# A scan and a mixer on one core: V in one transfer, and the first 150 steps in another order

## The chip, the core and the metric

The kernel runs on one core of a Trainium2 chip. Its engines each work through a queue of their own: TensorE (PE, with its weight loads shown as PEld), VectorE (DVE), ScalarE (ACT), GpSimd (POOL), and SyncE (SP), which here only issues transfers between memory and the on-chip buffers. An instruction starts when it is at the head of its engine's queue and what it waits for has happened. The metric is the device time of one execution in microseconds, as the median of a few runs.

## What is computed

A state-space scan over 4 batches of 8 heads (768 positions, 32 channels, 16 states) gives y. The mixer then takes y as 4 x 768 x 256.

```python
for c in range(nc):                                  # chunks of 32 positions
    L = exp(cum_i - cum_j) * causal
    y[c] = (C B^T * L) @ x + (C @ state) * exp(cum)
    state = exp(sum(la)) * state + sum_j B_j x_j exp(cum_last - cum_j)
h = x.transpose(0, 2, 1) @ U @ V                     # the mixer's x is y; rank 32 over the 768 positions
u = x + h.transpose(0, 2, 1)
out = u + maximum(u @ w_ch1, 0) @ w_ch2              # 256 -> 1024 -> 256
```

The weights U, V, w_ch1 and w_ch2 arrive as 64-bit numbers and are turned into 32-bit ones on the chip.

## The kernel before

The scan goes by pairs: a pair is 256 positions of one batch, so there are 12 pairs, three to a batch. Pairs 0, 1 and 2 make up batch 0. The mixer of batch 0 can begin when all three are through.

The order of all work is written out by hand: the string PLAN (line 40) is a list of 650 words, and the function follow issues what each word stands for, in that order. No scheduler moves anything afterwards, so the place of a word sets the place of its instructions in every engine's queue, its transfers in SP's queue included. The words that matter here, k being a pair:

- b, x, L, B, X: loads of B and C (bc) and of x of a pair; w and W: loads of a block of w_ch1 or w_ch2; Z and z: loads of V and of U. For a word that begins with B, X, w or L, the first load is held until the last VectorE instruction issued before it has run.
- Q, P: the product of bc with the decays (BC), on POOL for pairs 1 to 3, on DVE for the others. T, V: transposes of BC on PE, and ScalarE copies of them into T and Cm.
- g: the gram products on PE (line 537 for pairs 0 to 2, 547 for the others). m, M: their masks, m for the first two banks, M for the last two; in pairs 0 to 2 the fourth bank goes through ACT (line 563) and POOL.
- s: the state products (line 598). u: the running state S on DVE, and after its second call Sm (line 626), on POOL for pairs 0 to 3.
- n: y's part within the chunk (lines 694 and 704). i, j: y's part from the state (line 672), which needs Sm. y: copies of y into yT. t, O and o: transposes of yT and copies into ytok.
- c0 to c9: conversion of a weight block, four steps each, spread over DVE and ACT (lines 442 and 444). c1 converts U and V together; c0 and c2 give the first quarter of w_ch1, c4, c5 and c3 the others.
- p, q, a: the mixer's low-rank part: p multiplies ytok with U (line 751), q spreads the result (line 759) and makes ps, v makes V's spread form Vs (line 902), a adds h to yT (line 769, then four DVE additions for batch 0).
- U: the first w_ch1 products of batch 0 (line 797, "plain", w1f and yT). F: filler products on PE (line 148) that nothing reads.

Three rules set the waits. PSUM has eight banks, handed out in the order of the words, so a product can wait for a bank until an earlier tile in it has been read. Buffers in the pools raw and att are handed round in the same way. And the loads carry eight completion semaphores in turn, so a load is issued only when the eighth load before it has landed.

Of the kernel before, what the change touches and what calls it, by code (L numbers as in the profile page):

```python
# [39 lines left out]
PLAN = (  # L40
# [46 lines left out]
def kernel(  # L87
# [28 lines left out]
    P = 128  # L116
    NB, NH, S, D = x.shape
    N = B.shape[-1]
    NC = S // P
    NPR = NC // 2  # L120
    DM = NH * D
    RK = moe_U.shape[1]
# [7 lines left out]
    Q = 32  # L130
# [27 lines left out]
    class Kept:  # L158
# [6 lines left out]
        def __getattr__(self, name):  # L165
# [16 lines left out]
        out=a_sb,  # L182
        in_=a.rearrange("(g b) h (c s) -> g (b h c) s", g=2, s=P).rearrange(
            "g r s -> r g s"))
# [4 lines left out]
    def hold(load, until):  # L189

        tc.add_manual_dep(load.ins, until.ins.name, mybir.DependencyInfo(
            mybir.DependencyClass.Sync, mybir.DependencyReason.DATA))

    def begin(**kwargs):
        op = nc.sync.dma_start(**kwargs)  # L195
        if until:
            hold(op, until.pop())
# [26 lines left out]
    UV = const.tile([P, 2, NC * RK], FP32)  # L224
# [8 lines left out]
    w2 = [const.tile([P, NM, DM], FP32R, name=f"w2{i}") for i in range(2)]  # L233
    weights = {}
# [7 lines left out]
    def words_of(dst):  # L242
        p, i, j = dst.shape
        t = raw.tile([P, 2 * WCOLS], INT32, tag="words", name="words", bufs=NWORDS)
        return t[:p, :2 * i * j]
# [11 lines left out]
    U2, V2, w12, w22 = (w.bitcast(INT32) for w in (moe_U, moe_V, moe_w_ch1, moe_w_ch2))  # L257
# [2 lines left out]
    w13 = w12.rearrange("(c p) m -> p c m", p=P)  # L260
    own = {}

    def load_v():
        own["UV"] = words_of(UV)
        weights[1] = UV, own["UV"]
        for q in range(4):
            begin(out=own["UV"][ts(q, Q), 2 * NC * RK:], in_=V2[:, ts(q, 2 * NC * RK)])

    def load_u():
        begin(out=own["UV"][:, :2 * NC * RK].rearrange("p (c r) -> p c r", c=NC),  # L270
                          in_=U2.rearrange("(c p) r -> p c r", p=P))

    def load_w(n):
        if n < 2:
# [13 lines left out]
    def load(k):  # L288
        if k < NB * NPR:
            load_bc(k)  # L290
            load_x(k)

    loads = dict(B=load_bc, X=load_x, w=load_w, b=lambda k, p: load_bc(k, (p,)),
                 x=lambda k, c: load_x(k, (c,)), W=load_w, Z=lambda n: load_v(),
                 z=lambda n: load_u())
    for word in LOADS.split():
        loads[word[0]](*(int(v) for v in word[1:].split(".")))
# [36 lines left out]
    for half in range(2):  # L334
        both = sides[:, half].rearrange("p (g s r) -> p s g r", g=2, s=2)
        for s in range(2):
            nc.gpsimd.tensor_scalar(
                out=both[:, s], in0=same[:, None, :].to_broadcast([P, 2, Q]),
# [10 lines left out]
    for g in range(2):  # L349
# [3 lines left out]
        out=la.rearrange("p b c h -> p b h c"),  # L353
# [577 lines left out]
    def ytokens_kept(k):  # L931
# [9 lines left out]
                 v=spread)  # L941
# [51 lines left out]
```

## Time and profile before

| what | us |
|---|---|
| median of 3 runs | 218.69 |
| lowest and highest run | 217.45 and 219.20 |
| the profiled execution, its own time | 216.94 |
| its span, first to last instruction | 215.1 |

The span is what the views below divide up; the profiled execution's own time has 1.84 us around it. The profiled execution is 0.8% under the median of the runs. Busy times overlap, so they don't add up to the span. In a row of the timeline the two numbers ahead are the start and the length in microseconds, and the brackets at its end hold the engine's idle time before it and what ended it.

### The profile page before, as it was taken

Reading aid. Unit: us, or ns where it says so; the run is one execution under the profiler, and the core shown is the slowest. Engines: PE = TensorE matmul, PEld = TensorE weight load, DVE = VectorE, ACT = ScalarE, POOL = GpSimd, SP = SyncE. Lnnn points to the kernel's source line nnn. Section 1 sums busy time; section 2 is a strip of 40 time slices with the busy share of each in tenths; the row PEclk is TensorE's granted clock in tenths of the full one; section 3 lists DMA queues with packets and bytes.
Section 4 is the critical chain, followed back from the end, with each engine's and each line's share of the span. In section 5 each row is a group of like instructions: output and inputs, shape, how many; then the busy total and the mean of one; then the engine's idle time right before and its main releaser. Section 6 shows DMA issues by size and latency. Waiting matters only on the chain.

```text
span 215.1 us, 6853 instructions
## 1 busy us (share of the span) xinstructions
PE 207.0 (96%) x2912; PEld 180.8 (84%) x2912; DVE 161.3 (75%) x334; ACT 119.9 (56%) x273; POOL 14.5 (7%) x46
## 2 busy tenths in 40 slices
PE   7998699999999999999999999999999999999993
PEld 4666465666676989999899999998999999999993
DVE  4679499999999999968977594497347756636942
ACT  3566567896847695655275527433646357357120
POOL 7463210000000000000000000000000000000000
PEclk9999999999999999999999999999999999999999
DMA  5987899998850035002061010100001000100012
GB/s 87 142 184 106 120 202 316 155 265 110 109 80 3 2 66 111 0 3 76 3 81 21 24 49 3 49 27 6 6 0 49 0 27 0 49 29 0 0 50 100
DMA packets 69519, 14.57 MB, mean 68 GB/s; under 512 B 63792, under 2 KB 67696, under 8 KB 69488
## 3 DMA queue, kind: packets, MB, share of 16 engines
q1 hardware_dynamic: 69488, 14.13, 33.6%
q8 instruction: 23, 0.38, 0.8%
q14 instruction: 8, 0.07, 0.1%
HBM read 10.98 MB, written 3.15 MB: 66 GB/s over the span
## 4 chain that ended last, share of the span: by engine, by line
PE 84%; SPq 5%; DMA 4%; DVE 2%; issue 2%; ACT 1%; DVEq 0%
PE x L797 31%; PE z L797 24%; PE y L797 12%; SPq L195 5%; PE y L704 3%; PE y L672 3%; DMA words<-in_moe_w_ch_dram 3%; PE x L547 2%; PE w L728 2%; PE w L506 2%; DMA bc<-in_C_dram 2%; PE w L598 1%; PE w L751 1%; PE z L547 1%; DVE M L169 1%
## 5 line engine op out<-in xcount | busy, mean ns | idle before, releaser
L169 DVE SCALAR_TENSOR_TENSOR words<-words 128x768 fp32r<-128x768 f32 (+6 forms) x48 | 38.0, 818 | 0.7 <-PE y L797 0.5
L797 PE MATMUL z<-u,w 128*128 128x384 f32 x144 | 32.0, 341 | 0.0
L797 PE MATMUL x<-u,w 128*128 128x384 f32 x144 | 31.7, 338 | 0.0
L797 PEld LDWEIGHTS z<-u,w 128*128 128x128 f32 x144 | 24.3, 188 | 0.3 <-issue 0.2
L797 PEld LDWEIGHTS x<-u,w 128*128 128x128 f32 x144 | 24.3, 188 | 0.2
L802 ACT ACTIVATE x<-x 128x384 f32<-128x384 f32 (+1 forms) x32 | 14.3, 448 | 18.1 <-PE x L797 18.1
L802 ACT ACTIVATE z<-z 128x384 f32<-128x384 f32 (+1 forms) x28 | 12.8, 461 | 16.6 <-PE z L797 16.1
L169 DVE SCALAR_TENSOR_TENSOR words<-x,words 128x384 fp32r<-128x384 f32 x24 | 13.1, 553 | 8.7 <-ACT words L831 8.6
L169 DVE SCALAR_TENSOR_TENSOR words<-z,words 128x384 fp32r<-128x384 f32 x24 | 12.9, 552 | 8.9 <-ACT words L831 8.8
L797 PE MATMUL y<-w,words 128*128 128x256 f32 x144 | 19.3, 281 | 0.0
L797 PEld LDWEIGHTS y<-w,words 128*128 128x128 f32 x144 | 18.4, 189 | 0.1
L797 PE MATMUL x<-w,words 128*128 128x256 f32 x128 | 18.3, 281 | 0.0
L797 PE MATMUL x<-w2c,words 128*128 128x256 f32 x96 | 17.6, 317 | 0.0
L797 PEld LDWEIGHTS x<-w,words 128*128 128x128 f32 x128 | 17.0, 188 | 0.2
L797 PEld LDWEIGHTS x<-w2c,words 128*128 128x128 f32 x96 | 14.9, 189 | 1.1
L831 ACT ACTIVATE words<-x 128x384 fp32r<-128x384 f32 x24 | 11.7, 491 | 6.0 <-PE x L797 5.9
L831 ACT ACTIVATE words<-z 128x384 fp32r<-128x384 f32 x24 | 11.6, 492 | 3.0 <-PE z L797 3.0
L169 DVE SCALAR_TENSOR_TENSOR S<-S,kept,w 128x64 f32<-128x64 f32 x40 | 11.1, 278 | 1.6
L797 PE MATMUL z<-yT,w1f 128*128 128x384 f32 x32 | 11.7, 495 | 0.1
L797 PE MATMUL x<-yT,w1f 128*128 128x384 f32 x32 | 11.1, 489 | 0.0
L672 PEld LDWEIGHTS y<-T,Sm 32*64 32x64 f32 x352 | 8.1, 131 | 2.7 <-issue 2.1
L797 PE MATMUL y<-w2c,words 128*128 128x256 f32 x72 | 10.3, 282 | 0.0
(170 smaller groups left out, 398.4 us busy)
## 6 DMA issues: line engine op xcount, KB each, us to landing
words<-in_moe_w_ch_dram SPq DMA_DIRECT2D x7, 512.0 KB, 6.8
x<-in_x_dram SPq DMA_DIRECT2D x24, 128.0 KB, 3.6
out_dram<-ytok SPq DMA_DIRECT2D x24, 128.0 KB, 1.7
bc<-in_B_dram SPq DMA_DIRECT2D x24, 64.0 KB, 3.0
bc<-in_C_dram SPq DMA_DIRECT2D x12, 128.0 KB, 3.1
words<-in_moe_w_ch_dram SPq DMA_DIRECT2D x2, 256.0 KB, 5.5
words<-in_moe_V_dram SPq DMA_DIRECT2D x4, 48.0 KB, 4.8
words<-in_moe_U_dram SPq DMA_DIRECT2D x1, 192.0 KB, 5.0
```

The lines of the kernel that those rows point to most:

```text
L169: self.last = call(*args, **kwargs)
L195: op = nc.sync.dma_start(**kwargs)
L506: nc.tensor.transpose(out=tp[:, i, v], in_=s["BC"][:, i, c + v].rearrange("p h n -> p (h n)"), identity=ident)
L547: nc.tensor.matmul(out=g[r][cols, c], lhsT=s["T"][rows, 0, c, cols], rhs=s["Cm"][rows, :, :, ts(2 * c + p, Q)].rearrange("r v t i -> r v i ...
L598: nc.tensor.matmul(out=s["A"][p][ts(r, Q), v], lhsT=s["BC"][half, 0, v, 2 * r:2 * r + 2].rearrange("p h n -> p (h n)"), rhs=x_sb[k][half, ...
L672: product = nc.tensor.matmul(out=y[at][ts(r % 2, H), c, ts(p, H)] if light else y[p][ts(r % 2, H), r // 2, c], lhsT=own[ts(r, Q)], rhs=s[" ...
L704: product = nc.tensor.matmul(out=y[p][ts(i, Q), n, c], lhsT=x_sb[k][half, c, h], rhs=s["M"][half, h // 2, c, h % 2], start=fresh(k, p, [i] ...
L728: nc.tensor.transpose(out=t[:, c, g], in_=yT[b][:, g, ts(2 * q + c, P)], identity=ident)
L751: nc.tensor.matmul(out=p[ts(i % 4, Q), h], lhsT=U_sb[:, c], rhs=ytok[b][:, c, h], start=i < 4, stop=True, skip_group_check=True)
L797: nc.tensor.matmul(out=t, lhsT=lhsT, rhs=rhs, start=start, stop=True, skip_group_check=True)
L802: nc.scalar.activation(t, t, AF.Copy, scale=1.0 + EPS)
L831: nc.scalar.activation(gs[j, m // 2][0][:, m % 2], t, AF.Relu, scale=NEAR)
```

## The change

The table of words keeps its 650 words. The words that differ in place begin with the 40th and end with the 210th; nothing is added or taken out. In addition V, which was loaded by four transfers of 32 partitions each, is loaded by one transfer to 128 partitions, so that the program has 96 loads and stores in place of 99. A small function makes the buffer that U and V share, so that either load can come first.

```diff
-    'V1.1.2 b4.0 g0 M0 g1 m0 M1 V2.1.2 F2.1 V2.0.2 s1 b4.1 n0 m1 c2 i0 b4.2 j0 u1.0 b5.1 c0 u1.1 '
+    'V1.1.2 g0 b4.2 b4.1 m0 b4.0 b5.1 M0 g1 M1 m1 V2.1.2 s1 V2.0.2 g2 M2 u1.0 u1.1 c0 w3 P3 b5.2 '
...
+    def words_uv():
+        if "UV" not in own:
+            own["UV"] = words_of(UV)
+            weights[1] = UV, own["UV"]
+        return own["UV"]
+
     def load_v():
-        own["UV"] = words_of(UV)
-        weights[1] = UV, own["UV"]
-        for q in range(4):
-            begin(out=own["UV"][ts(q, Q), 2 * NC * RK:], in_=V2[:, ts(q, 2 * NC * RK)])
+        v = words_uv()[:, 2 * NC * RK:]
+        begin(out=v, in_=V2.rearrange("r (q c) -> q r c", q=4))
 
     def load_u():
-        begin(out=own["UV"][:, :2 * NC * RK].rearrange("p (c r) -> p c r", c=NC),
-                          in_=U2.rearrange("(c p) r -> p c r", p=P))
+        begin(out=words_uv()[:, :2 * NC * RK].rearrange("p (c r) -> p c r", c=NC),
+              in_=U2.rearrange("(c p) r -> p c r", p=P))
```

Line numbers of the changed kernel are higher by four behind this place: 537 becomes 541, and so on.

The loads on SP, where V is issued (x here is that of pair 2, bc that of pair 3):

```order
 L195 DMA words<-in_moe_w_ch_dram 128x2x256 x2
-L195 DMA words<-in_moe_V_dram 32x384 x4
+L195 DMA words<-in_moe_V_dram 128x1x384
 L195 DMA x<-in_x_dram 128x8x32
 L195 DMA bc<-in_B_dram 128x8x16
```

Four rows of V become one, in the same place. All that follows stands three places nearer the head of the queue. Further on, the loads of later pairs and of the weight blocks change places among themselves.

VectorE from the first updates of the state S on, through the masks of pairs 0 to 2 (words<-x and words<-z), the states of pairs 1 and 2 and the first conversions. Before:

```order
L169 SCALAR_TENSOR_TENSOR S<-S,kept,w 128x64 x3
L169 TENSOR_TENSOR words<-z,lower 128x512
L169 TENSOR_TENSOR words<-x,lower 128x512 x2
L169 TENSOR_TENSOR words<-z,lower 128x512
L169 TENSOR_TENSOR words<-x,lower 128x512 x2
L169 TENSOR_SCALAR words<-words 128x256 x2
L169 SCALAR_TENSOR_TENSOR S<-S,kept,w 128x64 x2
L169 TENSOR_SCALAR words<-words 128x256 x2
L169 SCALAR_TENSOR_TENSOR S<-S,kept,w 128x64 x2
L169 TENSOR_TENSOR words<-z,lower 128x512
L169 TENSOR_TENSOR words<-x,lower 128x512 x2
L169 SCALAR_TENSOR_TENSOR S<-S,kept,w 128x64 x3
```

The same stretch now:

```order
L169 SCALAR_TENSOR_TENSOR S<-S,kept,w 128x64 x3
L169 TENSOR_TENSOR words<-x,lower 128x512 x2
L169 TENSOR_TENSOR words<-z,lower 128x512 x2
L169 TENSOR_TENSOR words<-x,lower 128x512 x2
L169 TENSOR_TENSOR words<-z,lower 128x512
L169 SCALAR_TENSOR_TENSOR S<-S,kept,w 128x64 x4
L169 TENSOR_SCALAR words<-words 128x256 x2
L169 TENSOR_TENSOR words<-x,lower 128x512 x2
L169 TENSOR_SCALAR words<-words 128x256 x2
L169 SCALAR_TENSOR_TENSOR words<-words 128x256 x2
L169 SCALAR_TENSOR_TENSOR S<-S,kept,w 128x64 x3
```

The first mask of pair 2 stands ahead of the four state updates of pair 1, and the last state updates of pair 2 (x3) stand behind three rows of conversions and not between them.

TensorE in the same stretch, from behind the grams of pair 2 to the state products of pair 3 (y<-words,x is n, y<-T,Sm is i and j, w<-ident,BC the transposes of pair 3, x, w and z<-ident,yT those of yT). Before, where n and half of the i and j products of pair 0 stand ahead of those grams:

```order
L694 MATMUL y<-words,x 32x128 x16
L672 MATMUL y<-T,Sm 64x64 x8
L598 MATMUL w<-x,BC 32x64 x12
L728 MATMUL x<-ident,yT 128x128 x4
L672 MATMUL y<-T,Sm 64x64 x8
L694 MATMUL y<-words,x 32x128 x16
L672 MATMUL y<-T,Sm 64x64 x16
L506 MATMUL w<-ident,BC 128x128 x4
L728 MATMUL w<-ident,yT 128x128 x4
L598 MATMUL w<-x,BC 32x64 x16
```

And now:

```order
L698 MATMUL y<-words,x 32x128 x32
L676 MATMUL y<-T,Sm 64x64 x28
L602 MATMUL w<-x,BC 32x64 x12
L732 MATMUL x<-ident,yT 128x128 x4
L698 MATMUL y<-words,x 32x128 x16
L510 MATMUL w<-ident,BC 128x128 x2
L676 MATMUL y<-T,Sm 64x64 x16
L148 MATMUL x<-one 128x256
L510 MATMUL w<-ident,BC 128x128 x2
L732 MATMUL w<-ident,yT 128x128 x4
L602 MATMUL w<-x,BC 32x64 x16
```

The grams of pair 2 come ahead of all y products, the products of pairs 0 and 1 follow in one piece, and half of the transposes of pair 3 stand ahead of pair 2's last products; a filler product (L148) that stood much earlier is put between.

14 rows, old and new, of the table PLAN are left out of this document.

## The prediction

> **What bounds the kernel now.** I read the page's head first, then busy time by windows, then the chain of waits up to the first w_ch1 products, then the timeline of each engine from 10 to 33 us.
>
> ```profile
> span 215.1 us, 6853 instructions
> ...
> PE 207.0 (96%) x2912; PEld 180.8 (84%) x2912; DVE 161.3 (75%) x334; ACT 119.9 (56%) x273; POOL 14.5 (7%) x46
> ```
>
> ```profile
> 15.00:20.00 5.00, 4.24 (x148) 3.03 (x140) 4.45 (x14) 2.67 (x8) 1.51 (x3) 1.00 0.69 99
> 20.00:25.00 5.00, 3.81 (x107) 2.92 (x105) 2.33 (x8) 2.24 (x6) 1.72 (x2) 1.00 0.75 125
> 25.00:30.00 5.00, 3.97 (x101) 2.24 (x86) 4.55 (x15) 3.76 (x10) 0.62 (x1) 1.00 0.97 165
> 30.00:32.60 2.60, 2.56 (x81) 2.01 (x80) 2.51 (x7) 1.93 (x7) 0.10 (x1) 1.00 1.04 224
> 32.60:210.00 177.40, 177.36 (x2296) 160.42 (x2297) 137.38 (x265) 101.17 (x224) 0.84 (x8) 1.00 0.25 53
> ```
>
> Columns: the window, its length, busy PE, PEld, DVE, ACT, POOL, then granted clock, DMA share and GB/s. From 32.6 us to 210 us TensorE is idle for 0.04 us at the full clock. What it has to do there isn't changed, so that stretch keeps its length unless a new wait enters it, and what can be won lies before it: between 15 and 32.6 us TensorE is idle for 0.76 + 1.19 + 1.03 + 0.04 = 3.02 us. The question is when the dense stretch begins. The chain of waits shows what it begins behind:
>
> ```profile
> 10.52 5.51 DMA words<-in_moe_w_ch_dram
> ...
> 18.55 3.54 DMA bc<-in_C_dram
> 22.10 2.20 issue
> 24.30 0.53 ACT words L442
> ...
> 32.64 1.56 PE z L797 x4
> ```
>
> SP waits until 16.03 for the first w_ch1 block, since the second half of pair 2's x is the eighth load after it. Then come pair 3's loads, of which C lands at 22.09, then U, and at 24.30 ScalarE starts to convert U and V (the 2.20 us "issue" is it standing there). The plain w_ch1 products begin at 32.64. So the first 32 us are a race of loads, not of TensorE.
>
> **The change, part by part.** *V as one transfer.*
>
> ```profile
> 11.66 2.69 SPq L195 DMA_DIRECT2D words<-in_moe_V_dram  x4
> 14.39 0.43 SPq L195 DMA_DIRECT2D x<-in_x_dram  x1
> ...
> 19.18 0.58 SPq L195 DMA_DIRECT2D words<-in_moe_U_dram  x1
> ```
>
> ```profile
> words<-in_moe_U_dram SPq DMA_DIRECT2D x1, 192.0 KB, 5.0
> ```
>
> Four issues took 2.69 us; one takes 0.43 to 0.58 by its neighbours, and I take 0.55. All loads behind it move up by 2.1 us, x of pair 2 to 12.2. They are also three places nearer in the turn of eight semaphores: x's second half and pair 3's B and C now wait for bc and x loads that have long landed, so C can be issued after four loads of 0.58, at 14.5 in place of 18.55, and U waits for the first w_ch1 block (16.03) and is issued there in place of 19.18. By the same times to landing C lands at 18.1 at the earliest and U at 21.1. At the latest nothing is gained, 22.1 and 24.2, since the 16 DMA engines were also 0.69 busy there and take the bytes in order. I take the middle for C, 20, and 22 for U; up to about 22 either is free, for the reason that follows.
>
> *The grams of pair 2 ahead of the y products, their first mask ahead of pair 1's states, conversions ahead of pair 2's states.*
>
> ```profile
> 15.71 0.48 PE L537 MATMUL x<-Cm,T 32*64 32x256 f32 x1
> ...
> 17.86 1.08 PE L694 MATMUL y<-words,x 128*32 128x128 f32 x32 [0.76 <-DVE S L169]
> ...
> 21.69 0.78 PE L672 MATMUL y<-T,Sm 32*64 32x64 f32 x32
> 23.37 0.66 PE L506 MATMUL w<-ident,BC 128*128 128x128 f32 x4 [0.90 <-POOL BC L490]
> ```
>
> ```profile
> 14.59 0.67 ACT L516 ACTIVATE Cm<-x,slot 128x128 f32<-128x128 f32 x2
> ...
> 25.84 0.60 ACT L510 COPY T<-w 128x512 f32<-128x512 f32 x1
> 26.31 0.86 ACT L516 ACTIVATE Cm<-w,slot 128x256 f32<-128x256 f32 x2
> ```
>
> ```profile
> 14.43 1.28 DVE L169 TENSOR_TENSOR words<-x,lower 128x512 int32<-128x512 int32 x2
> 16.05 0.50 DVE L169 TENSOR_SCALAR words<-words 128x256 int32<-128x256 int32 x2 [0.34 <-DMA words<-in_moe_w_ch_dram]
> ...
> 17.95 0.68 DVE L169 TENSOR_TENSOR words<-z,lower 128x512 int32<-128x512 int32 x1
> 18.55 1.28 DVE L169 TENSOR_TENSOR words<-x,lower 128x512 int32<-128x512 int32 x2
> 19.90 0.92 DVE L169 SCALAR_TENSOR_TENSOR S<-S,kept,w 128x64 f32<-128x64 f32 x3
> ...
> 29.72 0.75 DVE L169 SCALAR_TENSOR_TENSOR words<-words 128x256 f32<-128x256 f32 x2
> ...
> 46.97 1.30 DVE L169 SCALAR_TENSOR_TENSOR S<-S,kept,w 128x64 f32<-128x64 f32 x4
> ```
>
> ```profile
> 20.91 0.62 POOL L626 TENSOR_TENSOR Sm<-S,own 128x192 f32<-128x192 f32 x1 [1.22 <-DVE S L169]
> 22.22 1.10 POOL L490 TENSOR_TENSOR BC<-bc,F 128x512 f32<-128x512 f32 x1 [0.70 <-DMA bc<-in_C_dram]
> ```
>
> The grams need Cm, which ScalarE has ready at 15.26; with the y products of pair 0 behind them TensorE has nothing in the meantime and loses about 0.9 us that it had filled. They start at 15.3 and end by 16.7: before it was 15.71 to 17.10, which is 17.86 less the wait of 0.76, with other products between, so 1.4 is a high price. VectorE, done with six masks at 15.71, now waits 1.0 for them. From 16.7 it has one mask (0.68), four states (1.30), two conversion rows (0.50 each), two masks (1.28), a third conversion row (0.75) and three states (0.92): 5.9 us as rows, and 5.75 with the 0.1 that consecutive rows overlap, so pair 2's states are done at 22.45 and not at 20.82. POOL's Sm follows at 23.1. Pair 3's BC stands ahead of it on POOL: with C at 20 it runs to 21.1 and hides, and only from C at 22 on does it hold Sm. The last half of pair 2's y products goes from 23.1 to 23.6, 1.1 us later than before (21.69 + 0.78 = 22.47).
>
> What is won back is behind that. Before, T3's transposes ended at 24.03, but their copy on ScalarE began at 25.84, behind the conversion of U that began at 24.30. Now U has landed by 22, VectorE comes to it at 22.5, and ScalarE is through with it by 23.6, under pair 2's products. The filler and T3's second half end at 24.4, the copies take 1.33 (25.84 to 27.17), and pair 3's grams start at 25.8 in place of 27.2: **1.4 us earlier**.
>
> *From there to the plain products* the same instructions run as before: four masks, V's split, BC of pair 4, a conversion, ps, the additions to yT. BC of pair 4 moves from behind ps to ahead of it, but both lay before the additions, so the stretch of 5.4 us (27.2 to 32.64) stays, and the products begin at 31.2. BC of pair 4 needs its loads by 29; they move up with the queue.
>
> *In the dense stretch* the order changes up to the 210th word. One place can give time back: pair 5's state products take the bank that t3's transposes had, behind a ScalarE copy that comes later among the new conversions.
>
> ```profile
> 46.46 0.59 ACT L733 COPY ytok<-w 128x512 f32<-128x512 f32 x1
> ```
>
> Nothing waits there now, so the price is between 0 and that copy's 0.59, and I take 0.4, nearer the upper end, since ScalarE has two conversion steps ahead of it. The x and w loads of later pairs are issued earlier than before or held by the same releases; I cost them at nothing, and their cover is the lead that they had. Sum: -1.4 + 0.4 = -1.0 us. The span goes from 215.1 to 214.1, the profiled execution from 216.94 to 215.9, and as a median, which stands at 218.69 against that execution, to 217.7.
>
> **The rivals.** *V on few engines.* The one transfer reads from memory in 4 blocks of 32 rows, where every load before has 32, 96 or 128 as its outermost count. If the four blocks mean four DMA engines, their share of V is 48 KB each and not 12.
>
> ```profile
> GB/s 164 246 246 266 225 205 205 184 287 266 266 266 297 297 266 317 358 358 369 389 420 338 246 328 328 287 185 246 215 185 144 308 174 154 51 82 21 51 21 82
> ```
>
> That is 13 to 15 us. At the 370 GB/s or so of V's time, 23 GB/s for an engine, V takes 2.1 us on them and not 0.5, and all loads behind wait for these four. C then lands about where it did, near 22.1; BC of pair 3 ends at 23.3, Sm behind it at 23.9, pair 3's grams start at 26.6, and of the 1.4 us 0.6 stay: -0.6 + 0.4 = -0.2, a median of 218.5. No run here has such a load, so nothing in the trace speaks for or against it. The Trainium skill states it as a rule: its page "DMA: Bandwidth & Descriptors", section "Why a DMA increments its semaphore by 16 and not by 1", says that a hardware-generated DMA uses the largest number of engines up to 16 that divides the slowest dimension of both sides, which for 4 and 128 gives the four lowest engines. By that rule the sum is this rival's, without it mine; the trace shows neither, and the chance below is for what it would cost here.
>
> *All of the idle goes.* If loads and copies fall so that TensorE never waits between 15 and 32.6 us, 3.0 us go: 215.7. Against it: the new gap of 0.9 at 14.4 and the later Sm.
>
> *Slower: a conversion between the additions.* The next w_ch1 block's first conversion row now stands on VectorE between the two pairs of additions to yT, at about 31.7; before it came behind all four. It needs the block's load.
>
> ```profile
> 27.01 0.75 SPq L195 DMA_DIRECT2D words<-in_moe_w_ch_dram  x1
> ```
>
> ```profile
> words<-in_moe_w_ch_dram SPq DMA_DIRECT2D x1, 512.0 KB, 5.1
> ```
>
> It landed at 32.1. If it comes no earlier, 0.4 is lost; each us past 31.7 holds VectorE's queue and then TensorE's third product. From a landing at 35 on the kernel is slower by 2.2 us, 220.9. I expect it near 30, since its place in the queue is ahead of two more loads than before.
>
> **How the numbers follow.** My forecast, 217.7: 0.45. V on few engines, 218.5: 0.25. No difference at all, 218.7, the gains and the new gap even: 0.07. All idle gone, 215.7: 0.13. Slower by a late block, 220.9: 0.10. About 1% is what a measurement of this kernel can tell from no change: the runs lie 0.8% apart. Below 216.5 lies the case of 215.7 and the edge of mine, 0.17; above 220.9 half and more of the slower case with longer waits, 0.10; within 1% the rest, 0.73. The range from 215.6 to 219.8 takes in the first four cases and leaves out the slower one and what lies beyond the gain.
>
> **What would show it.** Right: pair 3's C landed by 21 and U by 22; POOL's BC of pair 3 ahead of 22; a TensorE gap near 14.4 to 15.3; pair 3's grams near 25.8, the first plain product near 31.2, and no idle behind. Wrong: C at 22 or later with DMA engines unevenly busy (V on few engines); VectorE idle ahead of the row at 31.7 (late block); TensorE idle between 32 and 110 us, which would mean that the new order starves it where I assumed none.

## The result, and the profile after

| what | us |
|---|---|
| before, median of 9 runs (lowest to highest) | 218.69 (217.34 to 220.65) |
| after, median of 9 runs (lowest to highest) | 220.31 (218.79 to 221.42) |
| after / before, with its 95% interval | 1.0106 (1.0077 to 1.0135) |
| the profiled execution, after (before: 216.94) | 220.73 |
| its span, after (before: 215.1) | 219.0 |

The change costs 1.1% of the time: 1.6 us between the two medians, and 2.3 us by the ratio, which leaves out executions over 1.5% slower than the kernel's quickest, as every ratio below does. The forecast was a gain of 1.0 us. Here are the page's head and the busy time by windows after the change, with the windows and columns of the prediction:

```profile
span 219.0 us, 6852 instructions
...
PE 209.3 (96%) x2912; PEld 182.3 (83%) x2912; DVE 161.7 (74%) x334; ACT 120.4 (55%) x273; POOL 14.2 (6%) x46
```

```profile
15.00:20.00 5.00, 3.75 (x114) 2.55 (x106) 3.71 (x10) 2.64 (x9) 1.92 (x5) 1.00 0.60 105
20.00:25.00 5.00, 3.69 (x117) 2.71 (x117) 3.90 (x12) 2.52 (x7) 1.82 (x3) 1.00 0.87 140
25.00:30.00 5.00, 4.43 (x114) 3.23 (x118) 3.49 (x11) 3.78 (x9) 0.37 (x2) 1.00 0.73 99
30.00:32.60 2.60, 2.59 (x79) 1.61 (x75) 2.60 (x8) 1.70 (x6) 0.60 (x1) 1.00 1.05 227
32.60:210.00 177.40, 175.25 (x2306) 157.68 (x2300) 137.63 (x266) 102.42 (x226) 0.90 (x9) 1.00 0.26 54
```

From 32.6 to 210 us TensorE is now idle for 2.15 us in place of 0.04. Fixed windows mix causes, because this execution also reached its first gram product later (11.86 us, against 10.53), and that lies ahead of all that was changed. So I cut both executions at three events of the program instead: the first gram product of pair 0, that of pair 3, the first plain product, the end. Before, then after:

```profile
10.53:27.23 16.70, 13.79 (x392) 9.47 (x391) 11.86 (x31) 10.65 (x30) 6.92 (x13) 1.00 0.81 138
27.23:32.64 5.41, 5.26 (x143) 3.63 (x143) 4.98 (x15) 3.50 (x11) 0.72 (x2) 1.00 0.95 204
32.64:215.10 182.46, 179.22 (x2310) 162.08 (x2310) 138.38 (x267) 101.13 (x224) 0.84 (x8) 1.00 0.26 55
```

```profile
11.86:29.06 17.20, 14.07 (x391) 9.64 (x390) 12.01 (x30) 10.20 (x29) 6.81 (x13) 1.00 0.77 131
29.06:35.43 6.37, 5.31 (x142) 3.65 (x143) 5.23 (x15) 3.47 (x11) 0.72 (x2) 1.00 0.82 169
35.43:219.00 183.57, 179.47 (x2311) 162.10 (x2310) 138.31 (x267) 102.31 (x224) 0.79 (x8) 1.00 0.25 54
```

The three stretches grew by 0.50, 0.96 and 1.11 us, together 2.57, near the 2.3 of the ratio. Of this TensorE is idle for 0.22, 0.91 and 0.86 (length less busy PE), and busy longer by 0.28, 0.05 and 0.25. So the time isn't lost in one place. These are TensorE's waits in the profile after, first those from 14 to 34.4 us, then those from 34 to 205 us (us in total, how many, the longest):

```profile
PE w L510 <- POOL BC L494: 1.1, 1, 1.1
PE x L541 <- ACT Cm L520: 1.0, 1, 1.0
PE x L551 <- ACT Cm L520: 0.6, 1, 0.6
PE x L510 <- DVE words L169: 0.3, 1, 0.3
```

```profile
PE x L773 <- DVE w1f L169: 1.0, 1, 1.0
PE y L676 <- issue: 0.6, 1, 0.6
PE w L510 <- DVE M L169: 0.5, 1, 0.5
```

Before, the same view has nothing from 34 to 205 us. The last three rows are new: the product that makes ps and h (L773) just ahead of the plain products, pair 5's y products, and the transposes behind pair 5's masks.

### The profile page after: what moved, and what is told of

Same layout as the page of the kernel before. It is cut to its first block, busy times and chain, and to the rows that moved or that the text cites. A ratio compares the mean times of both kernels' runs of the same rounds, so it can differ in the third digit from the quotient of the medians.

```text
span 219.0 us, 6852 instructions
## 1 busy us (share of the span) xinstructions
PE 209.3 (96%) x2912; PEld 182.3 (83%) x2912; DVE 161.7 (74%) x334; ACT 120.4 (55%) x273; POOL 14.2 (6%) x46
## 4 chain that ended last, share of the span: by engine, by line
PE 78%; SPq 10%; DMA 4%; DVE 4%; issue 1%; ACT 1%; DVEq 0%; ACTq 0%
PE x L801 28%; PE z L801 23%; PE y L801 12%; SPq L195 10%; PE y L708 2%; DMA words<-in_moe_U_dram 2%; PE y L676 2%; PE x L551 2%; PE w L732 2%; DMA bc<-in_B_dram 2%; PE w L510 2%; DVE words L169 2%; PE w L755 1%; PE w L602 1%; DVE M L169 1%
## 5 line engine op out<-in xcount | busy, mean ns | idle before, releaser
L801 PE MATMUL x<-u,w 128*128 128x384 f32 x144 | 31.7, 338 | 0.0
L801 PE MATMUL z<-yT,w1f 128*128 128x384 f32 x32 | 11.9, 496 | 0.0
L676 PE MATMUL y<-T,Sm 32*64 32x64 f32 x352 | 10.5, 234 | 0.7 <-issue 0.6
L676 PEld LDWEIGHTS y<-T,Sm 32*64 32x64 f32 x352 | 8.5, 131 | 2.8 <-issue 1.9
```

What stands on the lines that cost most here:

```text
L676: product = nc.tensor.matmul(out=y[at][ts(r % 2, H), c, ts(p, H)] if light else y[p][ts(r % 2, H), r // 2, c], lhsT=own[ts(r, Q)], rhs=s[" ...
L801: nc.tensor.matmul(out=t, lhsT=lhsT, rhs=rhs, start=start, stop=True, skip_group_check=True)
```

## The experiments

Each ratio is against the kernel before on the same chip, with its 95% interval; a difference between two of the ratios carries the errors of both. "Old" and "new" order are those of before and after.

### V's form, or the order?

Old order with V in one transfer; new order with V in four:

```diff
 # e1: before, with
-        for q in range(4):
-            begin(out=own["UV"][ts(q, Q), 2 * NC * RK:], in_=V2[:, ts(q, 2 * NC * RK)])
+        begin(out=own["UV"][:, 2 * NC * RK:], in_=V2.rearrange("r (q c) -> q r c", q=4))
 # e2: after, with
-        v = words_uv()[:, 2 * NC * RK:]
-        begin(out=v, in_=V2.rearrange("r (q c) -> q r c", q=4))
+        v = words_uv()
+        for q in range(4):
+            begin(out=v[ts(q, Q), 2 * NC * RK:], in_=V2[:, ts(q, 2 * NC * RK)])
```

> The old order with V as the one transfer of 4 blocks of 32 rows. Theory F (the one transfer runs on four DMA engines and holds up the loads behind it; the new order by itself is worth what was forecast, about -1 us): the loads behind V land 1 to 2 us later than before, C of pair 3 at 23 to 24 and U at 25.3 to 26.2 us, and the time is 1.0 to 2.0 us over that of the kernel before. Theory O (the new order costs the time, V's form is neutral or a gain): C lands at 20 to 22, and the time is that of the kernel before or up to 0.5 us less.

> The new order with V in four transfers as before. Theory F: C of pair 3 near 22 and U near 24.2 us as before, the new order's own worth shows: 0 to 1 us below the kernel before. Theory O: the time of the changed kernel, 1 to 2 us over the kernel before, with TensorE idle behind 32.6 us as in the changed kernel.

And V in one transfer whose outermost count is 128 rows, in the new and the old order:

```diff
 # e3: after, and e4: before (there v is own["UV"][:, 2 * NC * RK:]), each with
+        begin(out=v, in_=V2.rearrange("r (q c) -> (r q) c", q=4))
```

> The new order with V in one transfer whose rows follow each other in memory as 128 rows of 384 words, so that V's rows come to other partitions than the ones that the mixer reads: the same bytes, one issue, another outermost count (the output is not that of the reference). Theory F: the transfer is spread over all engines and the loads behind it move up as the prediction had it, C of pair 3 at 18 to 21 and U at 21 to 23 us, and the time is 0.5 to 1.5 us below the kernel before. Theory O: C and U early too, but the time stays 0.5 us or more over the kernel before.

> The old order with V in one transfer of 128 rows of 384 words, again on other partitions than the mixer reads (the output is not that of the reference). Theory F: loads about 2 us earlier than before; ScalarE's conversion of U no longer waits for a load, and the time is 0 to 1 us below the kernel before. Theory O says the same of this one; it is the fourth cell of order against form, and tells whether the two add.

| run | order | V | ratio |
|---|---|---|---|
| e1 | old | one transfer, 4 blocks | 1.0027 (0.9998 to 1.0055) |
| e2 | new | four transfers | 1.0146 (1.0114 to 1.0179) |
| e3 | new | one transfer, 128 rows | 1.0110 (1.0077 to 1.0142) |
| e4 | old | one transfer, 128 rows | 0.9962 (0.9937 to 0.9986) |
| after | new | one transfer, 4 blocks | 1.0106 (1.0077 to 1.0135) |

Whatever V's form, the new order costs 0.8% to 1.5%, and by itself (e2) all of the loss. V's form is worth between -0.4% and +0.3% and not always the same way. (The profiled execution of e1 had a granted clock of 0.663 and isn't used.) The rival that V's few DMA engines cost the time falls as the main cause, although in the profile after the loads did go by it (below).

### Where in the order?

All of these have V in four transfers. c1 takes the new order up to pair 3's grams and the old from there on; c2 the reverse; d1 has the old order up to the first plain product; h3 is before with the words between pair 3's grams and the plain products alone as in the new order.

```diff
 # c1: the words of after up to 'O2.1 o2', then
+'c2 x4.1 w6 g3 M3 m3 v0 c2 p0 i3 q0 v1 B6 v2 P4 ...' and on as before
 # c2: the words of before up to 'c1 u3.1 O2.1', then
+'o2 g3 M3 m3 p0 v0 P4 i3 c2 q0 v1 v2 L9 v3 ...' and on as after
 # d1: the words of before up to 'T4 T4 w8 c4 c4', then
+'L9 P5 U0.0.1 U0.0.0 ...' and on as after
 # h3, against before:
-'v0 c2 p0 i3 q0 v1 B6 v2 P4 c2 n3 v3 a0.0 a0.1 R0 c4 c4 T4 T4 w8 c4 c4 U0.0.1 U0.0.0 P5'
+'v0 P4 c2 p0 i3 q0 v1 B6 v2 c2 n3 v3 T4 a0.0 T4 c4 w8 a0.1 P5 U0.0.1 c4 c4 c4 R0 U0.0.0'
```

> V in four transfers; the new order up to the grams of pair 3, the old order of what is left behind that. Theory E (early: the cost of the new order lies ahead of pair 3's grams, in VectorE's chain to pair 2's states and in TensorE's new gaps): nearly all of the 1.4% of the full new order, 217.6 us or more where the kernel before has 215.1 of span, ratio 1.010 to 1.015. Theory L (late: the cost lies behind pair 3's grams, in the additions to yT with the conversion between them and in the order of the first products): ratio within 0.3% of the kernel before. By the traces so far I expect about 1.3 us early (ratio 1.006) and the rest late.

> V in four transfers; the old order up to the grams of pair 3, the new order of what is left behind that. Theory E: within 0.3% of the kernel before. Theory L: ratio 1.010 to 1.015. By the traces so far I expect about 1.2 us (ratio 1.0055): 0.4 from the grams of pair 3 to the first plain product, since TensorE then waits 0.5 us for VectorE ahead of the first products of L769, and the rest behind it.

> V in four transfers, the old order up to the first plain product, the new order of what is left behind it (L9 then stands behind B6). Splits the late part, which cost 0.92% with the cut at pair 3's grams. If the loss lies between pair 3's grams and the first plain product (BC of pair 4 ahead of ps, a conversion between the additions, and L9 ahead of B6): within 0.3% of the kernel before. If it lies behind the first plain product: 1.006 to 1.010.

> The kernel before, V in four transfers, with the new order in one place only, from the masks of pair 3 to the first plain products: BC of pair 4 (P4) ahead of ps, and half of pair 4's transposes ahead of the first products of L769 and the first conversion step of the next w_ch1 block between the additions to yT (L9 stays behind B6). From the cuts so far this place is worth 0.4% (0.92 less 0.5): ratio 1.003 to 1.005. If L9 ahead of B6 or the w loads made that difference, it is within 0.2%.

| run | what is new | ratio |
|---|---|---|
| c1 | up to pair 3's grams | 1.0037 (1.0006 to 1.0068) |
| h3 | from there to the plain products | 1.0034 (0.9999 to 1.0068) |
| c2 | all behind pair 3's grams | 1.0092 (1.0060 to 1.0123) |
| d1 | all behind the first plain product | 1.0050 (1.0017 to 1.0084) |

c1 and c2 add up to 1.29%, where the whole order cost 1.46% (e2). c2 less d1 leaves 0.42% for the middle, and h3 measured 0.34% for it directly. So the loss is in three parts of about 0.4%, 0.4% and 0.5%, or 0.8, 0.8 and 1.1 us of 218, each with an interval of some 0.3% to either side. For c1, c2 and d1 the measured ratio lies outside the ranges of both theories: the loss is neither all early nor all late. The cut by events in the profile gave 0.50, 0.96 and 1.11. Both ways say that no part costs it all. That the sizes are alike is in part luck, because a word can cost time in another stretch than its own: in c1's profile pair 3's grams come only 0.09 us later than before, and the stretch behind them, whose words are the old ones there, takes 6.36 us in place of 5.41; in h3's profile that stretch, with the new words, takes 5.53. (The profiled execution of d1 was disturbed, its span 683.6 us, and isn't used.)

### Single mechanisms, one at a time

Pair 1's states and two conversion steps are put ahead of pair 2's first mask (c3); on top of that, pair 2's grams go back behind the first y products (c4); and L9 goes back to its old place (a1, a2):

```diff
 # c3, against after (V in four transfers):
-'V2.0.2 g2 M2 u1.0 u1.1 c0 w3 ... y0.1 c0 y1.0'
+'V2.0.2 g2 u1.0 c0 u1.1 c0 M2 w3 ... y0.1 y1.0'
 # c4, against c3:
-'V2.0.2 g2 u1.0 c0 u1.1 c0 M2 w3 P3 b5.2 n0 n1 m2 i0 j0 y0.0'
+'V2.0.2 u1.0 c0 u1.1 c0 w3 P3 n0 i0 g2 M2 j0 b5.2 n1 m2 y0.0'
 # a1, against after, and a2, against c3:
-'v1 v2 L9 v3 ... U0.1.5 T5 c5'
+'v1 v2 v3 ... U0.1.5 L9 T5 c5'
```

> The full new order with V in four transfers, but pair 1's states and the first two conversion rows' steps stand again ahead of pair 2's first mask on VectorE (u1.0 c0 u1.1 c0 ahead of M2). If VectorE's chain to pair 2's states is what costs early (its wait of 1.2 us for the grams, and conversion rows that take 0.7 to 1.0 us in place of 0.28 where they meet work on POOL), the rows fall into that wait and into a time when POOL is idle, pair 2's states come 1 to 2 us earlier, TensorE's wait for Sm goes, and the time is 0.7 to 1.2 us under that of the full new order (ratio 1.009 to 1.011 to the kernel before). If that chain is not the cause, it stays at 1.0146.

> As the one before, and besides pair 2's grams stand again behind the first y products of pair 0 on TensorE (n0 i0 ahead of g2, j0 behind its mask). If TensorE's new gap ahead of the grams (1.0 to 1.2 us) counts, another 0.5 to 1.2 us go, ratio 1.004 to 1.007. If it was only moved work and pair 3's grams wait for the loads anyway, nothing more goes.

> The changed kernel with one word moved: the loads of pair 9 (L9) stand again behind the loads of pair 6 (B6), at their old place behind U0.1.5. Theory Q (the queue: five loads of pair 9 ahead of pair 6's make VectorE wait 1.1 us for pair 6's B at 52 us, and TensorE 0.5 us behind it): pair 6's loads land 2 to 3 us earlier, that wait goes, and the time falls by 0.5 to 1.1 us, ratio 1.005 to 1.009 to the kernel before. If VectorE is so late that the loads don't matter, the time stays that of the changed kernel, 1.0106.

> As c3_states_before_mask (new order, V in four transfers, pair 1's states and first conversions ahead of pair 2's mask), with L9 behind B6 besides. There the first plain product came at 32.28 us, 2.0 us earlier than in the full new order, but 2.07 us of VectorE's wait for pair 6's B and 2.5 us of TensorE's idle time followed. Theory Q: these go and the early gain reaches the end: 2 us or more under c3, ratio 0.998 to 1.003 to the kernel before. If the gain is lost to something else behind the first plain product, ratio stays near 1.01.

c3 1.0110 (1.0064 to 1.0156), c4 1.0130 (1.0090 to 1.0170), a1 1.0100 (1.0063 to 1.0137), a2 1.0112 (1.0068 to 1.0157). a1 stays where after is (1.0106). c3, c4 and a2 have V in four transfers, so they are to be held against e2 (1.0146): they lie 0.2% to 0.4% under it, within the errors of both. For c3 that is the gain that was expected of it, but it isn't clear of noise. No edit moved the total by more than that, and c3's profile shows why a local gain need not. It reached the first plain product 21.82 us after pair 0's grams, 0.29 sooner than before and 1.75 sooner than after, and lost it all behind. Its timeline of VectorE has a wait for pair 6's B, and its waits of TensorE from 32 to 205 us show what that did:

```profile
52.08 0.69 DVE L169 TENSOR_TENSOR BC<-bc,F 128x512 f32<-128x512 f32 x1 [2.07 <-DMA bc<-in_B_dram]
```

```profile
PE w L511 <- DVE M L169: 1.3, 1, 1.3
PE y L709 <- DVE M L169: 0.5, 1, 0.5
PE y L677 <- issue: 0.3, 1, 0.3
PE w L603 <- ACT ytok L738: 0.2, 1, 0.2
```

The masks M of pair 5 stand on VectorE behind that BC, and TensorE stands behind the masks. The same chain is in the profile after: BC at 52.33 behind 1.10 of waiting, masks late, 0.54 on TensorE. With L9 back (a1) TensorE doesn't wait for M, and the ratio is still 1.0100; and e2 and c4, where L9 wasn't moved, don't show that wait either. The chain is real, but it is not what costs the time in every run.

Next come the filler (h1, h2), the first part mended (h4), and the order of the loads (k1, k2):

```diff
 # h1, against after:
-'V2.1.2 s1 V2.0.2 ... c0 F2.1 T3'
+'V2.1.2 F2.1 s1 V2.0.2 ... c0 T3'
 # h2, against before:
-'V2.1.2 F2.1 V2.0.2 s1 ... c1 T3 t1'
+'V2.1.2 V2.0.2 s1 ... c1 F2.1 T3 t1'
 # h4, against c1: both edits of c3 and h1
 # k1, against after, and k2, against h4: w5, w6, x4.1, x4.0 and X5 at
 # their old places, and in k1 L9 behind X6 (the lines are k1's; in k2
 # x4.1 and w6 leave a place ahead of g3)
-'y1.0 c2 w2 c0 s2 u2.0 u2.1 X5 O0.0 ... T3 i2 j2 y2.1 y2.0 x4.0 c0'
+'y1.0 c2 w5 w2 c0 s2 u2.0 u2.1 O0.0 ... T3 x4.1 i2 j2 y2.1 y2.0 c0'
-'c1 w5 c1 t1 s3 u3.0 u3.1 ... i3 w6 x4.1 c2'
+'c1 c1 t1 s3 w6 u3.0 x4.0 X5 u3.1 ... i3 c2'
```

> The changed kernel with one word moved: the filler product F2.1 stands again between the two transposes of pair 2 (V2.1.2 and V2.0.2), ahead of pair 1's state products. Theory W (the filler covered the time in which TensorE waits for pair 1's x and for pair 2's Cm; without it TensorE is idle for 1.2 to 2.7 us between 13 and 16.5 us, and in 10 of 21 runs of the new order the granted clock had a window of 3.4 us at one half, against 6 of 53 of the old): the share of runs with a granted clock of 0.993 or less falls to 2 in 10 or fewer, and the time by 0.3 to 0.8%, ratio 1.003 to 1.008. Rival: the filler only fills, and the wait behind it is the same; clock windows rarer perhaps, the ratio stays at 1.010.

> The kernel before with that one word moved the other way: F2.1 between the two halves of pair 3's transposes, as in the changed kernel; V in four transfers. Theory W: windows at half clock in 3 of 10 runs or more, and ratio 1.003 to 1.008. Rival: within 0.2% of the kernel before.

> V in four transfers, the new order up to pair 3's grams and the old one behind (1.0037 as it was), with two changes: F2.1 at its old place, and pair 1's states and the first two conversion steps ahead of pair 2's first mask. If the early order cost its 0.4% by the lost filler and by VectorE's chain to pair 2's states, it is 0.996 to 1.000 here, a version that beats both; if not, 1.003 or more.

> The changed kernel with five load words at their old places (w5, w6, x4.1, x4.0 and X5 in their old order ahead of pair 3's grams, and L9 behind X6), so that SP's queue has the old order of loads again, while the engines keep the new order of work and V stays one transfer. Theory S (SP's queue: in the new order the x loads of pairs 4 and 5, which wait for a buffer until 38.3 us, stand ahead of the two blocks of w_ch2, which were issued at 30.4 and 31.7 us before and are at 38.6 and 40.2 now; the last two blocks land at 55.6 in place of 47.8, and conversions and products behind them go late): those two issues come back to 32 us or earlier, the span from the first plain product to the end falls from 183.6 to 182.5 or less, and the time by 0.4 to 0.9%, ratio 1.002 to 1.006. If the blocks' lateness is covered and the order of the engines' work costs by itself: 1.009 or more.

> h4_early_new_mended (new order up to pair 3's grams with F2.1 and pair 1's states mended, old order behind, V in four transfers, 1.002) with w5, w6, x4.1, x4.0 and X5 at their old places. There pair 3's grams began at 26.24 us, 1.0 earlier than before, and the chain of waits names a w_ch2 block issued at 37.70 and landed at 43.06 behind which the gain went. Theory S: the block lands by 41, and the gain of 0.5 to 1.2 us reaches the end: ratio 0.994 to 0.998, better than both kernels. Otherwise 1.000 or more.

h1 1.0114 (1.0073 to 1.0155), h2 1.0020 (0.9988 to 1.0053), k1 1.0105 (1.0063 to 1.0147): neither the filler nor the loads' order carries the loss. h4, 1.0020 (0.9986 to 1.0053), is before within its interval, where c1 had been 1.0037, too near to say that the edits mended anything. In its profile pair 3's grams start 15.54 us after pair 0's, 1.16 sooner than before: here the gain that I had forecast (1.4) is seen. 0.7 of it goes in the dense stretch, which takes 183.16 in place of 182.46. Its longest wait there is 0.4 us, and the chain of waits has a w_ch block behind it:

```profile
PE z L803 <- ACT words L450: 0.4, 1, 0.4
```

```profile
37.70 5.36 DMA words<-in_moe_w_ch_dram
```

That block lands at 43.06, and ScalarE's conversion waits for it. Moving the w and x loads to their old places should have kept the gain. k2 did that: 1.0022 (0.9991 to 1.0053), its grams at 17.04. A miss: the gain of h4's profile isn't seen there, and by the times neither kernel is better than before.

### V on another queue

```diff
 # f2, against before: Z0 ahead of K0, and
-            begin(out=own["UV"][ts(q, Q), 2 * NC * RK:], in_=V2[:, ts(q, 2 * NC * RK)])
+            nc.scalar.dma_start(
+                out=own["UV"][ts(q, Q), 2 * NC * RK:], in_=V2[:, ts(q, 2 * NC * RK)])
```

> The old order with V's four transfers issued by ScalarE in its idle time ahead of the step K0, so that SP has four issues less and the loads behind V move up as they do with one issue, and the loads spread over all DMA engines. If V's four issues on SP are what keeps the loads late, this is worth what V in 128 rows was worth with the old order, ratio 0.994 to 0.998, with the right output. If ScalarE's issues (some 0.5 us each) or V's early bytes delay the first pairs, it is 1.000 to 1.005.

A miss. In its profile, TensorE waits between 10 and 16 us, where before it waits for nothing:

```profile
PE x L508 <- POOL BC L492: 2.9, 1, 2.9
PE x L539 <- ACT Cm L518: 0.2, 1, 0.2
```

The shorter SP queue gives back less: from pair 0's grams to the first plain product this profile takes 0.88 us less than before. The ratio is 1.0077 (1.0028 to 1.0126). The granted clock was 0.977 to 0.985 in 8 of its 12 runs, and their times, 222.45 to 226.48 us, are not in that ratio.

Of all these only e4 is faster than before, by 0.4%, and it puts V's rows into other partitions than the mixer reads. None that could replace before beats it.

## Why the prediction was wrong

In short: the 1.4 us ahead of pair 3's grams weren't won, and the two stretches behind them, which I had left at their length but for 0.4, grew by 2.1 us in the profile. Step by step:

**"All loads behind it move up by 2.1 us": failed.** SP's timeline after, from V's issue on:

```profile
12.60 0.71 SPq L195 DMA_DIRECT2D words<-in_moe_V_dram  x1
13.36 0.44 SPq L195 DMA_DIRECT2D x<-in_x_dram  x1
13.84 0.58 SPq L195 DMA_DIRECT2D bc<-in_B_dram  x1
14.46 4.29 SPq L195 DMA_DIRECT2D x<-in_x_dram  x1
...
20.46 0.58 SPq L195 DMA_DIRECT2D bc<-in_C_dram  x1
21.09 0.67 SPq L195 DMA_DIRECT2D words<-in_moe_U_dram  x1
```

The issue itself was near the forecast (0.71 for 0.55). But SP then stood 4.29 us in the issue of x, until 18.75, and pair 3's C landed at 23.64 (forecast 20, the rival 22.1) and U at 26.09. Of that, 1.33 us is the later start of this execution; without it C landed at 22.3 and U at 24.8. V's 128 rows moved between 15.00 and 18.49 us, never more than 6 at a time, where before they were mostly done in 13.62 to 15.3, up to 14 at a time. Its completion shows 5 updates, one at 13.71 and four from 18.70 to 18.98, where every other load has 16. That is what the rival said. By the Trainium skill's page "DMA: Bandwidth & Descriptors", section "Why a DMA increments its semaphore by 16 and not by 1", 4 against 128 gives four engines; the trace agrees, with the four late updates. So the rival was right about the loads, and I gave it the smaller chance. With 128 rows (e3) C landed at 21.47 and U at 22.19, or 20.3 and 21.0 without that execution's later start of 1.20 us, as I had forecast for a quick V, and yet the kernel cost as much. The step is wrong, and it held up pair 3's grams in after (next but one), but it isn't what the loss as a whole is made of.

**The grams of pair 2, the wait for them: right.** They began 4.90 us after pair 0's (forecast 4.77), TensorE lost 0.26 + 0.99 (forecast 0.9), VectorE waited 1.18 (forecast 1.0).

**"Pair 3's grams start at 25.8 ... 1.4 us earlier": failed.** After has them 0.50 later relative to pair 0's; even e3, with its early loads, has them 16.63 us behind, 0.07 earlier than before. One term was mis-sized. I priced a pair of conversion rows on VectorE at 0.50. In e3 the loads were as early as forecast and this term decided. The rows of e3, then those of POOL beside them:

```profile
19.79 0.93 DVE L169 TENSOR_SCALAR words<-words 128x256 int32<-128x256 int32 x2
...
21.84 1.24 DVE L169 TENSOR_SCALAR words<-words 128x256 int32<-128x256 int32 x2
```

```profile
19.95 0.62 POOL L630 TENSOR_TENSOR Sm<-S,own 128x256 f32<-128x256 f32 x1 [0.22 <-DVE S L169]
21.63 1.10 POOL L494 TENSOR_TENSOR BC<-bc,F 128x512 f32<-128x512 f32 x1 [1.05 <-DMA bc<-in_C_dram]
```

Both pairs ran while POOL worked and took 1.17 more than priced; alone, such a pair took 0.49 in h4. So pair 2's states were done 12.85 us after pair 0's grams and not 11.9, and from there to pair 3's grams it went as forecast, but 0.4 slower. In after it was the loads. Only the first pair of rows ran beside POOL (0.94; the second took 0.48), and the states were done 12.12 us after pair 0's grams, 0.2 later than forecast. But POOL's BC waited for C, and ScalarE's conversion for U:

```profile
23.80 1.10 POOL L494 TENSOR_TENSOR BC<-bc,F 128x512 f32<-128x512 f32 x1 [3.07 <-DMA bc<-in_C_dram]
```

```profile
26.19 0.55 ACT L446 ACTIVATE words<-words 128x384 f32<-128x384 uint32 x1 [2.46 <-DMA words<-in_moe_U_dram]
```

TensorE waited 1.1 for that BC (the first row of its waits), Sm behind BC ended 13.50 us after pair 0's grams (forecast 12.6), and ScalarE came to the copies of pair 3's transposes at 27.67, behind U. This is the path of the rival of V on few engines. The two things explain why the gain stayed out. What turned it into a loss of 0.4% (c1) isn't settled: h4 changed three things of the early part and both signs lie within its interval, and c1's own profile loses its time behind pair 3's grams, in a wait of 0.93 (below).

**"The stretch of 5.4 us stays": failed.** It takes 6.37 in after, 0.96 more. h3 measured 0.34% for the order of these words alone, but its interval just touches zero, and its profile shows only 0.12 us of it. In after the loss is the wait of 1.0 of L773. Its row names w1f, which the product doesn't read; it reads Vs and ps. In k1, where the same product waits 1.07 until 32.89, the rows are:

```profile
31.45 0.43 DVE L169 TENSOR_TENSOR ps<-w,ps 64x256 fp32r<-64x256 f32 x1
```

```profile
32.00 0.19 PEld L773 LDWEIGHTS x<-Vs,ps 128*128 128x128 f32 x1 [0.42 <-ACT Vs L910]
```

ps was done at 31.88 and Vs loaded at 32.19, 0.70 before the product began. The traces point to TensorE's own instructions. They came in 23 packets of 16 KB (queue q8, "instruction", of the page), and the trace has some 5890 records of TensorE's products, weight loads and waits, so a packet holds 256 of them. The product that waits in after and in k1 is record 1217, counted by start from 0. In c1, k2 and f2, where the words of this stretch are the old ones, TensorE waits 0.93, 0.54 and 1.36 at record 1217 or 1218 as well, in front of other products, and the view names no releaser. The rows of c1 and f2:

```profile
33.58 0.44 PE L775 MATMUL z<-Vs,ps 128*128 128x384 f32 x1 [0.93 <-issue]
```

```profile
34.33 0.44 PE L508 MATMUL w<-ident,BC 128*128 128x128 f32 x2 [1.36 <-issue]
```

In these five profiles, and in c3 and e2 (0.64 and 0.53 of waiting), the product began 1.24 to 1.53 us after the end of the last such packet, which was at 33.17 in after. Before, that packet ended at 29.84 and TensorE came to record 1217 at 31.96, without a wait. So the wait of L773 is most likely one for instructions that came late, which can fall on old words as well as on new ones. It stays an inference: no run moved the place where a packet begins, why a packet is late isn't shown, and in e3 a wait of 0.52 came 2.06 us behind the packet and doesn't fit. Between profiles with the new words there the wait varies from none (c2) to 1.07.

**"That stretch keeps its length" and "I cost them at nothing": failed.** The dense stretch grew by 1.1 us in the profile and by 0.50% in d1. The sum had +0.4 for pair 5's bank: that wait didn't occur in after (c3 shows 0.2 of such a wait, the last row of its waits). In its place stand the chain of pair 6's B, the wait of L676, and more time in products. The wait of L676, at 84.16, is again at the edge of a packet: record 2754, six times 256 behind the one of L773 give or take one, and 1.49 us after its packet ended. "The x and w loads of later pairs are issued earlier or held by the same releases" is where I looked least: two w_ch2 blocks went out at 38.56 and after in place of 30.36 and 31.74.

```profile
33.69 4.78 SPq L195 DMA_DIRECT2D x<-in_x_dram  x3
38.56 2.06 SPq L195 DMA_DIRECT2D words<-in_moe_w_ch_dram  x2
```

But k1 issued them at 32.14 and 33.25, its dense stretch took 182.62, and the ratio stayed 1.0105. The assumption was false; that it cost the time isn't shown.

**The slower rival** named one place, the conversion at 31.7 behind a late block. It ran at 35.76, its block had landed at 33.08, and it waited for nothing. A slower outcome came, but by other ways than the one that I had priced.

What stays open: which waits make up each of the three parts, and how much of the loss in the runs without a profile is late instructions. Six kernels that undo something in the new order (c3, c4, a1, a2, h1, k1) stayed between 1.0100 and 1.0130, where the intervals are some 0.4% to either side, so none of the edits is seen to carry a part of it.

## What to carry to other kernels

A new order of many words in a hand-written schedule is many small changes at once; cut it by words at two or three events and time each part before arguing about mechanisms. A gain of 1 us at a milestone (c3, h4) is worth nothing until the stretch behind it is read too: what stands behind the early work in each queue was placed for the old time. And of moved words, price an instruction with what will run beside it: the conversion rows cost twice as much beside POOL. Before putting a wait down to the words around it, see whether it falls on the same record of the engine in kernels where other words stand there.

## What had not been expected of the hardware

One transfer of 192 KB in 4 blocks took 3.5 us for its rows, and SP then stood 4.29 us in the issue of x. With 128 rows it stood there too, for 2.98 us (e3). In the old order the 4 blocks cost only 0.27% (e1), within its interval.

In seven profiles TensorE waited 0.5 to 1.4 us at the place where, as far as the records tell, a new packet of 256 of its instructions begins (above).

VectorE's integer conversion row of 128 x 256 took 0.28 alone, 0.73 and 1.04 with POOL at work.

The granted clock fell to half for 3.4 us after short idle stretches. The rows of e2 show TensorE's idle before it, then the clock by windows:

```profile
14.39 0.46 PE L603 MATMUL w<-x,BC 64*32 64x64 f32 x32 [1.17 <-DVE words L169]
...
16.20 0.64 PE L542 MATMUL x<-Cm,T 32*64 32x256 f32 x2 [0.99 <-ACT Cm L521]
```

```profile
15.00:16.40 1.40, 0.41 (x10) 0.20 (x16) 0.57 (x1) 0.90 (x3) 0.00 (x0) 0.96 0.51 141
16.40:19.80 3.40, 3.40 (x68) 2.32 (x67) 1.44 (x4) 0.93 (x2) 0.79 (x2) 0.51 0.99 131
19.80:25.00 5.20, 4.98 (x162) 3.72 (x150) 5.13 (x14) 2.98 (x9) 2.12 (x4) 1.00 0.81 127
```

2.2 us of idle in two pieces stand ahead of it. A mean granted clock of 0.993 or less, which one such window makes, was in 13 of 114 runs of before, in 29 of 66 runs with the new early order and the filler late, and in 6 of 30 with the filler back (1 of 6 in h1, 1 of 12 in h4, 4 of 12 in k2). The gap ahead of pair 2's grams, and the filler that no longer stands there, would explain that, but it isn't shown: in h2, the old order with the filler late, it was 1 of 12. It isn't the whole loss: the runs above 0.993 alone have medians of 220.37 in after against 218.69 of all runs before, 219.02 in a1 against 217.27, 219.24 in k1 against 217.5, 218.45 in e3 against 216.63, all some 0.8% slower. Over all runs the medians are 0.7% to 0.9% slower in after, a1 and k1, and 1.2% in e3, where only 2 of 6 runs are above 0.993, so the windows can have added a few tenths of a per cent at most.
